# Clustered attention in slots of three steps instead of two: six PSUM banks for scores, one for all preparation

## The chip, the cores and the metric

One Trainium2 chip, one NeuronCore of it. The time is the device time of one execution in microseconds (us), the median of three runs. The engines named below are TensorE (PE; its weight loads are listed as PEld), VectorE (DVE), ScalarE (ACT), GpSimd (POOL, here a queue for transfers) and SyncE (SP, the other queue for transfers). [...]

## The reference, cut to what matters

```python
# q, k, v: (4, 8, 768, 64); centroids: (8, 16, 64); all float32
q_assign = argmax(einsum('bhsd,hcd->bhsc', q_n, c_n), -1)     # nearest centroid of each query
k_assign = argmax(einsum('bhsd,hcd->bhsc', k_n, c_n), -1)     # and of each key
mask   = q_assign[:, :, :, None] == k_assign[:, :, None, :]
scores = where(mask, q @ k^T / sqrt(64), -1e9)
attn   = softmax(scores);  x = attn @ v                       # then to (4, 768, 512)
xn  = layernorm(x) * g_ln
out = x + relu(xn @ w_ch1) @ w_ch2                            # 512 -> 2048 -> 512
```

## The kernel before, in words

**Work.** The 32 heads (4 batches of 8) are taken two at a time: 16 pairs. A pair has 768 queries in two halves of 384 (`g`) and 768 keys in six blocks of 128 (`c`), so 12 *steps* (`g`, `c`). For one step, `scores` (L373) forms a tile of 128 keys by 2 heads by 384 queries in PSUM: two bf16 matmuls lay down the mask ("far" where clusters differ), four float32 matmul records add q.k, and ACT takes the exponential into an SBUF tile `e` (L384). `weigh` (L394) multiplies the step's `e` with v into the pair's accumulator (L401), and DVE adds the `e` tiles up into `es` (L415, L418), the denominators of the softmax.

**Order.** PE, DVE and ACT run in the order written out by hand (`manual_schedule`, L606 to L670). The unit of that order is a *slot*: the score matmuls of the next two steps, then the weighing of the two steps before them; six slots are a pair. PSUM is split 4 + 1 + 3: `ps_s` holds two score tiles of two banks each, `ps_a` one accumulator, `ps_t` three banks for all else. All else is the preparation of later pairs and the finish of earlier ones:

- slot 1: `prep_sims(n+1)`, similarities of q and k to the centroids (PE L295), copied out by ACT (L304)
- slot 2: `prep_turn`, `prep_route`: transposed on PE (L311), arg-max as one-hot on DVE (L320, L322)
- slot 3: `prep_onehot`: one-hot transposed on PE (L337), `m` (L358 on ACT) and after each of the slot's score steps one `prep_mask` (L358 again)
- slot 5: `prep_transpose(n+2, ...)`: k turned by DVE (L273); q turned by PE (L278) with an ACT copy (L284) up to pair 6, by DVE from pair 7 (`TWICE = 7`). After each, the loads of pair n+3 into the same buffers are issued on the SP queue.

**Finish.** The result of a pair is divided by its denominators three stages later, because these must be spread over partitions through DRAM. `finish(n-1, 0)` in slot 0: PE sums `es` over partitions (L438), ACT copies (L446), POOL sends `flat` and fetches it back as `rdens` (L448, L449). `finish(n-1, 1)` in slot 3: DVE takes the reciprocal (L453), POOL writes `row` to DRAM (L455) and reads it back, broadcast, as `rb` (L463, two transfers). `finish(n-2, 2)` in slot 0 of the pair after: DVE multiplies `x` by `rb` (L470) and transposes (L477), SP stores. So from the reciprocal to its use the order leaves slots 3, 4, 5 and 0.

**Fillers on DVE.** In two slots of each of the first seven pairs and one slot of the later ones, a 512-column piece of the weights, which arrive as float64 words, is turned into float32: `split_weight` (three DVE instructions, L240 to L246) and, one slot later, `join_weight` (L255 to L260 and a POOL transfer L263), then the load of another piece. From pair 5 on, `extra` adds layer-norm work for the first batch of the second stage (L508, L509, L537, L539).

Second stage, from about 366 us on: the two layers of the feed-forward part as seven-product block multiplications (L711, L804). The change does not touch it.

Of the kernel before, what the change touches and what calls it, by code (L numbers as in the profile page):

```python
# [8 lines left out]
F32 = mybir.dt.float32  # L9
BF16 = mybir.dt.bfloat16  # L10
# [5 lines left out]
PSUM = bass.MemoryType.PSUM  # L16
# [3 lines left out]
def kernel(  # L20
# [35 lines left out]
    def pool(name, bufs, **kw):  # L56
        return stage.enter_context(tc.tile_pool(name=name, bufs=bufs, **kw))
# [5 lines left out]
    attn = pool("attn", 2)  # L63
    dram = ctx.enter_context(tc.tile_pool(name="dram", bufs=4, space=bass.MemoryType.DRAM))
    last = pool("last", 1)
    ps_s = pool("ps_s", 2, space=PSUM)
    ps_a = pool("ps_a", 1, space=PSUM)
    pools = {"t": pool("ps_t", 3, space=PSUM), "conv": conv}

    def ps(name, dt=F32, n=512):  # L70
        return pools["t"].tile([P, n], dt, tag="t", name=name)
# [3 lines left out]

    TWICE = 7

    blocks = {(n, name) for n in range(1, len(pairs)) for name in ("qk" if n >= TWICE else "k")}

    def load_blocks(n, name):  # L80
        b, pr = pairs[n]
# [44 lines left out]
    make_identity(nc, ident)  # L126
    identb = const.tile([P, P], BF16, name="identb")
    nc.gpsimd.tensor_copy(identb, ident)
    ones = const.tile([P, Q], F32, name="ones")
    nc.gpsimd.memset(ones, 1.0)  # L130
    rev = const.tile([P, NCL], F32, name="rev")
# [34 lines left out]
    def norm_centroids(part):  # L166
        if part == 0:
            nc.vector.tensor_tensor(c_sq, c_sb, c_sb, ALU.mult)
            nc.vector.tensor_reduce(c_ss, c_sq, AX.X, ALU.add)

            nc.vector.tensor_scalar_max(c_ss, c_ss, 2.0 ** -100)
        elif part == 1:
            nc.scalar.activation(c_nrm, c_ss, AF.Sqrt)
            nc.scalar.activation(warm, warm, AF.Exp, scale=0.0)
        else:

            nc.vector.reciprocal(c_tmp, c_nrm)
            nc.vector.scalar_tensor_tensor(
                out=c_tmp, in0=c_tmp, scalar=c_ss, in1=c_nrm, op0=ALU.mult, op1=ALU.add
            )  # L180
            nc.vector.tensor_scalar(c_nrm, c_tmp, 0.5, 1e-6, op0=ALU.mult, op1=ALU.add)
            nc.vector.reciprocal(c_tmp, c_nrm)
            nc.vector.tensor_scalar_mul(c_sb, c_sb, c_tmp)
# [5 lines left out]
    def turn_centroids():  # L189
        ct_ps = ps("ct_ps")  # L190
        nc.tensor.transpose(ct_ps[:D, : H * NCL], c_sb, ident[: H * NCL, : H * NCL])
        ct_v = ct_ps[:D, : H * NCL].rearrange("p (r j c) -> p r j c", j=2, c=NCL)
        for j in range(2):
            nc.vector.tensor_copy(cT[j * D : (j + 1) * D, :, j, :], ct_v[:, :, j, :])
# [70 lines left out]

    prepared = {n: {} for n in range(len(pairs))}

    def prep_transpose(n, side):
        src = loaded[n]["qk"[side]]
        t_sb = heads.tile([P, S], F32, tag=f"t{side}", name=f"t{side}")  # L270
        prepared[n][side] = t_sb
        if (n, "qk"[side]) in blocks:
            nc.vector.transpose(t_sb, src)  # L273
            return
        for g in range(NHALF):
            t = ps("qk_ps")
            for c in range(TH):
                nc.tensor.transpose(  # L278
                    t[:, c * P : (c + 1) * P],
                    src[:, g * TH + c, :, :].rearrange("p h d -> p (h d)"),  # L280
                    ident,
                )
            if n or g == side:
                nc.scalar.copy(t_sb[:, g * HC : (g + 1) * HC], t[:, :HC])  # L284
            else:
                nc.vector.tensor_copy(t_sb[:, g * HC : (g + 1) * HC], t[:, :HC])
# [20 lines left out]
    def prep_turn(n):  # L307
        sim_sb = prepared[n]["sim"]
        simT = ps("simT_ps")
        for c in range(TH):  # L310
            nc.tensor.transpose(  # L311
                simT[:, c * P : (c + 1) * P], sim_sb[:, c * P : (c + 1) * P], ident
            )
        prepared[n]["simT"] = simT
# [34 lines left out]
    def prep_mask(n, j):  # L349
        t, z = prepared[n]["oh"], mask[n % 2]  # L350
        src, dst = ((D, 0), (Q, D + Q))[j]
        src, dst = slice(src, src + NCL), slice(dst, dst + NCL)
        shade(n, z[dst], t[src, :S], src)
# [19 lines left out]
    def scores(i, first="mask", parts=("mask", "qk", "exp")):  # L373
        n, g, c = steps[i]
        st = prepared[n]
        if parts[0] == first:
            st["s", i] = ps_s.tile([P, 2, 512], F32, tag="s", name="s_ps")
        s = st["s", i]
        keys, cols = slice(c * P, (c + 1) * P), slice(g * HC, (g + 1) * HC)
        rows = [slice(j * D, (j + 1) * D) for j in range(2)]  # L380
        for part in parts:
            if part == "exp":
                e = attn.tile([P, 2, HC], F32, tag="e", name="e", bufs=5)
                nc.scalar.activation(e, s[:, :, :HC], AF.Exp, scale=SCALE)  # L384
                soft[i] = e
                continue
            for j in range(2):
                of_keys, of_queries = st["m"][j] if part == "mask" else [st[i][rows[j]] for i in (1, 0)]
                nc.tensor.matmul(  # L389
                    s[:, j, :HC], of_keys[:, keys], of_queries[:, cols],  # L390
                    start=part == first, stop=part != first, skip_group_check=True,
                )
# [186 lines left out]
    def put(n, slot, f, *args):  # L579
        extra.setdefault((n, slot), []).append(lambda: f(*args))  # L580

    put(5, 1, norm_load, 0)
    put(5, 2, rows_load, 0, 0)
    for t in range(NT):
        put(5 + (t + 1) // 2, (3, 5)[(t + 1) % 2], norm_rows, 0, t)
    put(9, 0, norm_stats, 0)
    put(9, 3, norm_stat_rows, 0)
    for i in range(2):
        for c in range(NDC):
            put(10 + 2 * i + c // 2, (2, 5)[c % 2], norm_apply, 0, i, c)  # L590
    put(14, 2, x_sum, 0, 1)
    put(14, 5, x_sum, 0, 2)
    put(15, 5, w1_sums, 0, 0, (0, 1))


    steps = [(n, g, c) for n in range(len(pairs)) for g in range(NHALF) for c in range(NT)]
    per = NHALF * NT
    slots = per // 2

    convert = {}  # L600
    for n in range(len(pairs)):
        for slot in (0, 3) if n < TWICE else (0,):
            convert[n, slot] = len(convert)
    order = {mybir.EngineType.PE, mybir.EngineType.DVE, mybir.EngineType.Activation}
    limit[0] = len(convert)
    with tc.manual_schedule(engines=order):  # L606
        norm_centroids(0)
        prep_transpose(0, 0)
        load(1, "q")
        norm_centroids(1)  # L610
        prep_transpose(0, 1)
        load(1, "k")
        norm_centroids(2)
        turn_centroids()
        prep_sims(0)
        prep_turn(0)
        scores(0, "qk", ("qk",))
        prep_route(0)
        load_weight(0)
        load_weight(1)  # L620
        prep_onehot(0)
        prep_mask(0, 0)
        prep_mask(0, 1)
        scores(1, "qk", ("qk",))
        scores(0, "qk", ("mask", "exp"))
        scores(1, "qk", ("mask", "exp"))
        prep_transpose(1, 0)
        load(2, "q")
        for u in range(len(pairs) * slots):
            n, slot = divmod(u, slots)  # L630
            nxt = n + 1 < len(pairs)
            if slot == 1:
                load(n + 1, "v")
            if u == 0:
                prep_transpose(1, 1)
                load(2, "k")
            if slot == 1 and nxt:
                prep_sims(n + 1)
            if slot == 2 and nxt:
                prep_turn(n + 1)  # L640
                prep_route(n + 1)
            if slot == 3 and nxt:
                prep_onehot(n + 1)
            if slot == 5 and n + 2 < len(pairs):
                prep_transpose(n + 2, 1)
                load(n + 3, "k")
                prep_transpose(n + 2, 0)
                load(n + 3, "q")
            for j in range(2):
                if 2 * u + 2 + j < len(steps):  # L650
                    scores(2 * u + 2 + j)
                if slot == 3 and nxt:
                    prep_mask(n + 1, j)
            if slot == 0 and n:
                finish(n - 1, 0)
            weigh(2 * u)
            weigh(2 * u + 1)
            if slot == (3 if nxt else 2) and n:
                finish(n - 1, 1)
            if slot == 0 and n > 1:  # L660
                finish(n - 2, 2)
            if slot == 5 and not nxt:
                finish(n - 1, 2)
            if (n, slot) in convert:
                split_weight(convert[n, slot])
            if (n, slot - 1) in convert:
                join_weight(convert[n, slot - 1])
                load_weight(convert[n, slot - 1] + 2)
            for job in extra.pop((n, slot), ()):
                job()  # L670

# [470 lines left out]
```

## Time and profile before

| | before |
|---|---|
| time, median of 3 runs | 952.06 us (951.9 to 952.77) |
| span of the profiled execution | 953.5 us |
| PE busy, instructions | 936.6 us (98%), 4614 |
| PEld busy | 574.5 us (60%) |
| DVE busy, instructions | 612.7 us (64%), 1105 |
| ACT busy | 347.6 us (36%) |
| DMA, mean busy share 0 to 100 us / 100 to 200 us | 0.6 to 0.9 / 0.88 |

A row of the costliest groups gives line, engine, operation, output<-inputs, shapes and count; then busy time and the mean of one; then the idle time of the engine just before these instructions and what ended it. In a timeline a row gives start, duration, engine, line and operation, and in brackets the idle time before it and who ended it. Ends of matmuls are modelled and overlap, so for PE the distance from start to start is the price of a block of work, not the sum of durations.

### The profile page before, as it was taken

What the parts mean: (1) busy time and instruction counts of PE and PEld (TensorE: products, weight loads), DVE (VectorE), ACT (ScalarE), POOL (GpSimd) and SP (SyncE); (2) the same over time, 40 slices, a digit from 0 to 9 for tenths busy, and PEclk for the clock granted to TensorE, in tenths of its full rate; (3) what the DMA queues carried; (4) which work ended last, traced back from release to release, by engine and by line L of the source; (5) the groups of instructions that cost most, each with busy time, mean ns of one, the idle gap of its engine ahead of it and who ended that gap; (6) DMA issues with size and microseconds to landing.
All of it is one profiled execution on the core that took longest, in us unless ns stands there. A gap on an engine that the chain in (4) does not pass through costs nothing.

```text
span 953.5 us, 12450 instructions
## 1 busy us (share of the span) xinstructions
PE 936.6 (98%) x4614; PEld 574.5 (60%) x4614; DVE 612.7 (64%) x1105; ACT 347.6 (36%) x555; POOL 79.0 (8%) x147
## 2 busy tenths in 40 slices
PE   7999999999999999999999999999999999999997
PEld 3444443444444444557887557887556887556886
DVE  4788888988888886799892436372445472344431
ACT  3666666677666663332001332001332000333000
POOL 2111111221111121110000000000000000000000
PEclk9999999999999999999999999999999999999999
DMA  8568889887877533564451002021001121000011
GB/s 175 122 150 192 194 176 205 189 194 153 178 149 158 132 69 100 137 146 144 134 159 39 1 0 78 23 89 45 0 1 58 41 84 51 1 0 7 29 45 35
DMA packets 178212, 92.48 MB, mean 97 GB/s; under 512 B 144224, under 2 KB 160720, under 8 KB 178144
## 3 DMA queue, kind: packets, MB, share of 16 engines
q1 hardware_dynamic: 168800, 76.20, 32.1%
q0 software_dynamic: 7744, 15.02, 7.9%
q8 instruction: 38, 0.62, 0.3%
q10 hardware_dynamic: 1600, 0.39, 0.2%
q14 instruction: 30, 0.25, 0.1%
HBM read 64.10 MB, written 19.10 MB: 87 GB/s over the span
## 4 chain that ended last, share of the span: by engine, by line
PE 90%; DVE 5%; issue 2%; DMA 2%; ACT 1%; POOL 0%; ACTq 0%; DVEq 0%; POOLq 0%
PE x_ps L804 17%; PE x_ps L711 16%; PE s_ps L389 15%; PE a_ps L401 12%; PE z_ps L804 9%; PE z_ps L711 8%; PE y_ps L804 4%; PE y_ps L711 4%; PE den_ps L438 1%; PE sim_ps L295 1%; DVE es L418 1%; PE simT_ps L311 1%; PE oh_ps L337 1%; PE qk_ps L278 1%; DMA rb<-row 1%
## 5 line engine op out<-in xcount | busy, mean ns | idle before, releaser
L384 ACT ACTIVATE e<-s_ps 128x768 f32<-128x768 f32 x192 | 151.6, 810 | 68.5 <-PE s_ps L389 67.7
L389 PE MATMUL s_ps<-t,t 64*128 64x384 f32 x768 | 156.5, 486 | 0.0
L401 PE MATMUL a_ps<-e,v_sb 128*64 128x384 f32 x768 | 144.8, 499 | 0.0
L418 DVE TENSOR_TENSOR es<-es,e 128x768 f32<-128x768 f32 x128 | 121.9, 952 | 24.0 <-ACT e L384 18.2
L401 PEld LDWEIGHTS a_ps<-e,v_sb 128*64 128x64 f32 x768 | 46.7, 136 | 87.7 <-issue 71.0
L731 DVE TENSOR_TENSOR h<-z_ps,u 128x384 f32<-128x384 f32 x64 | 35.6, 556 | 94.8 <-PE z_ps L711 71.5
L804 PE MATMUL x_ps<-w2t,h 128*128 128x256 f32 x384 | 84.5, 379 | 0.0
L389 PEld LDWEIGHTS s_ps<-t,t 64*128 64x128 f32 x768 | 69.0, 190 | 20.2 <-issue 18.7
L739 ACT ACTIVATE h<-h 128x384 f32<-128x384 f32 x96 | 49.6, 522 | 85.1 <-DVE h L731 85.1
L804 PEld LDWEIGHTS x_ps<-w2t,h 128*128 128x128 f32 x384 | 72.7, 190 | 10.1
L389 PE MATMUL s_ps<-m,mask 64*128 64x384 bf16 x192 | 62.9, 328 | 1.2 <-ACT e L384 1.0
L389 PE MATMUL s_ps<-mask,m 64*128 64x384 bf16 x192 | 62.7, 328 | 0.4 <-DVE mask L360 0.4
L726 ACT COPY u<-x_ps 128x384 f32<-128x384 f32 x64 | 30.6, 478 | 78.6 <-PE x_ps L711 78.6
L815 DVE TENSOR_TENSOR o_sb<-x_ps,xb 128x256 f32<-128x256 f32 x48 | 20.1, 420 | 51.3 <-PE x_ps L804 48.7
L726 ACT COPY p<-x_ps 128x384 f32<-128x384 f32 x32 | 14.9, 467 | 100.7 <-PE x_ps L711 100.7
L389 PEld LDWEIGHTS <-mask 64*128 64x128 bf16 x192 | 17.9, 93 | 54.5 <-issue 39.2
L711 PE MATMUL x_ps<-xt,ws 128*128 128x384 f32 x128 | 46.6, 487 | 0.8 <-DVE ws L574 0.8
L711 PE MATMUL x_ps<-xn,w 128*128 128x384 f32 x128 | 46.6, 487 | 0.6 <-ACT late L427 0.6
L711 PE MATMUL z_ps<-xt,ws 128*128 128x384 f32 x128 | 46.6, 487 | 0.0
L711 PE MATMUL z_ps<-xn,ws 128*128 128x384 f32 x128 | 46.5, 486 | 0.0
L711 PE MATMUL x_ps<-xn,ws 128*128 128x384 f32 x128 | 46.5, 486 | 0.0
L711 PE MATMUL x_ps<-xt,w 128*128 128x384 f32 x128 | 46.5, 486 | 0.0
(140 smaller groups left out, 1373.6 us busy)
## 6 DMA issues: line engine op xcount, KB each, us to landing
raw<-in_moe_w_ch_dram SPq DMA_DIRECT2D x32, 512.0 KB, 5.2
w<-tb POOLq DMA_DIRECT2D x32, 256.0 KB, 5.4
v_sb<-in_v_dram SPq DMA_DIRECT2D x32, 192.0 KB, 4.1
xn<-xT_d SPq DMA_DIRECT2D x16, 384.0 KB, 5.9
xr<-x_d SPq DMA_DIRECT2D x24, 256.0 KB, 3.2
xb<-x_d SPq DMA_DIRECT2D x48, 128.0 KB, 2.3
out_dram<-o_sb SPq DMA_DIRECT2D x48, 128.0 KB, 1.7
k_sb<-in_k_dram SPq DMA_DIRECT2D x62, 96.0 KB, 5.0
```

The costliest lines, as they stand in the source:

```text
L278: nc.tensor.transpose(t[:, c * P : (c + 1) * P], src[:, g * TH + c, :, :].rearrange("p h d -> p (h d)"), ident,)
L295: nc.tensor.matmul(sim[r : r + Q, :HC], cT[:, pr, :, :].rearrange("p j c -> p (j c)"), prepared[n][side][:, g * HC : (g + 1) * HC], start= ...
L384: nc.scalar.activation(e, s[:, :, :HC], AF.Exp, scale=SCALE)
L389: nc.tensor.matmul(s[:, j, :HC], of_keys[:, keys], of_queries[:, cols], start=part == first, stop=part != first, skip_group_check=True,)
L401: nc.tensor.matmul(acc[j * D : (j + 1) * D, :HC], loaded[n]["v"][:, j, c, :], e[:, j, :], start=(c == 0), stop=(c == NT - 1),)
L418: nc.vector.tensor_tensor(es, es, soft.pop(i), ALU.add)
L711: nc.tensor.matmul(bank[:, :HC], lhs[:, c, :], rhs[:, c, :], start=first and c == 0, stop=c == NDH - 1, skip_group_check=True,)
L726: nc.scalar.copy(t, bank[:, :HC])
L731: nc.vector.tensor_tensor(h, bank[:, :HC], other, ALU.add)
L739: nc.scalar.activation(h, h, AF.Relu)
L804: nc.tensor.matmul(bank[:, :MH], hidden[lhs + (c,)][:, tt * P : (tt + 1) * P], rhs[:, c, :], start=first and c == 0, stop=c == NFH - 1, sk ...
L815: nc.vector.tensor_tensor(o, bank[:, :MH], x, ALU.add)
```

## The change

The slot grows from two steps to three, so that a pair has four slots. To have three score tiles at once, `ps_s` takes six banks, and `ps_t` keeps one, so each piece of preparation waits until the one before it has been read out. The buffers of `e` go from five to seven. The work of the six slots is dealt onto four: similarities before the scores of slot 0, turning and arg-max after them; denominators (`finish 0`) in slot 1; one-hot and masks in slot 2; transposes for pair n+2 in slot 3, the PE transposes of q in two halves because only one bank is there. `finish(n-1, 1)` stays at slot 3 and `finish(n-2, 2)` at slot 0. Weight pieces are split in slots 1 and 2. Further, DVE turns pair 1's q too, the centroids' norms are finished earlier at the start and the exponential's table is loaded later, and 24 matmuls on zeros keep PE busy until the first q is there. The purpose is fewer changes between score and weighing work on PE, and a faster start.

```diff
-    ps_s = pool("ps_s", 2, space=PSUM)
+    ps_s = pool("ps_s", 3, space=PSUM)
...
-    pools = {"t": pool("ps_t", 3, space=PSUM), "conv": conv}
+    pools = {"t": pool("ps_t", 1, space=PSUM), "conv": conv}
...
-    blocks = {(n, name) for n in range(1, len(pairs)) for name in ("qk" if n >= TWICE else "k")}
+    blocks = {
+        (n, name) for n in range(1, len(pairs)) for name in ("qk" if n == 1 or n >= TWICE else "k")
+    }
...
-                e = attn.tile([P, 2, HC], F32, tag="e", name="e", bufs=5)
+                e = attn.tile([P, 2, HC], F32, tag="e", name="e", bufs=7)
...
-        for slot in (0, 3) if n < TWICE else (0,):
+        for slot in (1, 2) if n < TWICE else (1,):
...
+        idle = ps("idle_ps")
+        for _ in range(24):
+            nc.tensor.matmul(idle[:, :P], zeros, zeros, start=True, stop=True)
...
+        for side in (1, 0):
+            prep_transpose(1, side)
+            load(2, "qk"[side])
...
-            if slot == 1 and nxt:
+            if slot == 0 and nxt:
                 prep_sims(n + 1)
             if slot == 2 and nxt:
+                prep_onehot(n + 1)
+            if slot == 3 and n + 2 < len(pairs):
+                prep_transpose(n + 2, 1)
+                load(n + 3, "k")
+                prep_transpose(n + 2, 0, (0,))
+            for j in range(GROUP):
+                if GROUP * (u + 1) + j < len(steps):
+                    scores(GROUP * (u + 1) + j)
+                if slot == 2 and nxt and j < 2:
+                    prep_mask(n + 1, j)
+            if slot == 0 and nxt:
                 prep_turn(n + 1)
                 prep_route(n + 1)
...
+            if slot == (1 if nxt else 0) and n:
+                finish(n - 1, 0)
+            if slot == 3 and n + 2 < len(pairs):
+                prep_transpose(n + 2, 0, (1,))
                 load(n + 3, "q")
...
-            if slot == 0 and n:
-                finish(n - 1, 0)
-            weigh(2 * u)
-            weigh(2 * u + 1)
-            if slot == (3 if nxt else 2) and n:
+            for j in range(GROUP):
+                weigh(GROUP * u + j)
+            if slot == (3 if nxt else 1) and n:
                 finish(n - 1, 1)
             if slot == 0 and n > 1:
                 finish(n - 2, 2)
```

More of the change, by code (lines that the diff above doesn't have):

```diff
@@ L128 @@
     nc.gpsimd.tensor_copy(identb, ident)
+    zeros = const.tile([P, P], BF16, name="zeros")
+    nc.vector.memset(zeros, 0.0)
     ones = const.tile([P, Q], F32, name="ones")
@@ L173, in norm_centroids @@
             nc.scalar.activation(c_nrm, c_ss, AF.Sqrt)
-            nc.scalar.activation(warm, warm, AF.Exp, scale=0.0)
         else:
@@ L266, with prep_transpose @@
     prepared = {n: {} for n in range(len(pairs))}
-    def prep_transpose(n, side):
+    def prep_transpose(n, side, halves=range(NHALF)):
         src = loaded[n]["qk"[side]]
-        t_sb = heads.tile([P, S], F32, tag=f"t{side}", name=f"t{side}")
-        prepared[n][side] = t_sb
+        if 0 in halves:
+            prepared[n][side] = heads.tile([P, S], F32, tag=f"t{side}", name=f"t{side}")
+        t_sb = prepared[n][side]
         if (n, "qk"[side]) in blocks:
-            nc.vector.transpose(t_sb, src)
+            if 0 in halves:
+                nc.vector.transpose(t_sb, src)
             return
-        for g in range(NHALF):
-            t = ps("qk_ps")
+        if n == 0:
+            both = ps_s.tile([P, 2, 512], F32, tag="s", name="qk_ps")
+        for g in halves:
+            t = ps("qk_ps") if n else both[:, g]
             for c in range(TH):
@@ L282, in prep_transpose @@
                 )
-            if n or g == side:
+            if n or side == 0 or g == 1:
                 nc.scalar.copy(t_sb[:, g * HC : (g + 1) * HC], t[:, :HC])
@@ L582 @@
     put(5, 1, norm_load, 0)
-    put(5, 2, rows_load, 0, 0)
+    put(5, 1, rows_load, 0, 0)
     for t in range(NT):
-        put(5 + (t + 1) // 2, (3, 5)[(t + 1) % 2], norm_rows, 0, t)
+        put(5 + (t + 1) // 2, (1, 2)[(t + 1) % 2], norm_rows, 0, t)
     put(9, 0, norm_stats, 0)
-    put(9, 3, norm_stat_rows, 0)
+    put(9, 2, norm_stat_rows, 0)
     for i in range(2):
         for c in range(NDC):
[L590 to L593, printed above, removed]
+            put(10 + 2 * i + c // 2, (1, 2)[c % 2], norm_apply, 0, i, c)
+    put(14, 1, x_sum, 0, 1)
+    put(14, 3, x_sum, 0, 2)
+    put(15, 3, w1_sums, 0, 0, (0, 1))
     steps = [(n, g, c) for n in range(len(pairs)) for g in range(NHALF) for c in range(NT)]
     per = NHALF * NT
-    slots = per // 2
+    GROUP = 3
+    slots = per // GROUP
     convert = {}
     for n in range(len(pairs)):
-        for slot in (0, 3) if n < TWICE else (0,):
+        for slot in (1, 2) if n < TWICE else (1,):
             convert[n, slot] = len(convert)
@@ L610 @@
         norm_centroids(1)
+        norm_centroids(2)
         prep_transpose(0, 1)
         load(1, "k")
-        norm_centroids(2)
         turn_centroids()
+        nc.scalar.activation(warm, warm, AF.Exp, scale=0.0)
         prep_sims(0)
@@ L623 @@
         prep_mask(0, 1)
[L624 to L628, printed above, removed]
+        for i in range(1, GROUP):
+            scores(i, "qk", ("qk",))
+        for i in range(GROUP):
+            scores(i, "qk", ("mask", "exp"))
+        for side in (1, 0):
+            prep_transpose(1, side)
+            load(2, "qk"[side])
         for u in range(len(pairs) * slots):
@@ L633 @@
                 load(n + 1, "v")
-            if u == 0:
-                prep_transpose(1, 1)
-                load(2, "k")
-            if slot == 1 and nxt:
+            if slot == 0 and nxt:
                 prep_sims(n + 1)
             if slot == 2 and nxt:
+                prep_onehot(n + 1)
[9 more added lines that the diff above has]
+            if slot == 0 and nxt:
                 prep_turn(n + 1)
                 prep_route(n + 1)
[L642 to L647, printed above, removed]
-                load(n + 3, "q")
[L649 to L653, printed above, removed]
-            if slot == 0 and n:
-                finish(n - 1, 0)
-            weigh(2 * u)
-            weigh(2 * u + 1)
-            if slot == (3 if nxt else 2) and n:
+            if slot == (1 if nxt else 0) and n:
+                finish(n - 1, 0)
+            if slot == 3 and n + 2 < len(pairs):
+                prep_transpose(n + 2, 0, (1,))
+                load(n + 3, "q")
+            for j in range(GROUP):
+                weigh(GROUP * u + j)
+            if slot == (3 if nxt else 1) and n:
                 finish(n - 1, 1)
@@ L661 @@
                 finish(n - 2, 2)
-            if slot == 5 and not nxt:
+            if slot == 3 and not nxt:
                 finish(n - 1, 2)
-            if (n, slot) in convert:
-                split_weight(convert[n, slot])
             if (n, slot - 1) in convert:
@@ L668 @@
                 load_weight(convert[n, slot - 1] + 2)
+            if (n, slot) in convert:
+                split_weight(convert[n, slot])
             for job in extra.pop((n, slot), ()):
```

## The prediction

> **What bounds the kernel now.** I read the granted clock first (1.00 all through), then the busy tenths in 40 slices:
>
> ```profile
> PE   7999999999999999999999999999999999999997
> DVE  4788888988888886799892436372445472344431
> ```
>
> PE sets the time; DVE is at seven to nine tenths in the attention stage (to about 366 us). Then PE's timeline in a quiet pair (start, duration, what):
>
> ```profile
> 212.25 0.33 PE L389 MATMUL s_ps<-m,mask 64*128 64x384 bf16 x1
> ...
> 213.06 0.32 PE L389 MATMUL s_ps<-m,mask 64*128 64x384 bf16 x1
> ...
> 213.97 1.51 PE L401 MATMUL a_ps<-e,v_sb 128*64 128x384 f32 x8
> 215.41 0.33 PE L389 MATMUL s_ps<-m,mask 64*128 64x384 bf16 x1
> ```
>
> A slot of two steps is 215.41 - 212.25 = 3.16 us. The first step's scores are 0.81, the second's 0.91: 0.10 goes into the change to weighing. Weighing takes 1.44; its eight matmuls at the spacing of a step's four float32 score matmuls (0.645 for four) are 1.29, so the change back costs 0.15. Six slots are 18.96 us. Similarities add 0.78, turning 0.48, one-hot 0.44, denominators 0.78 (distances between block starts with and without them): 21.44, and the denominators' matmuls do come back every 21.46 us in most later pairs, every 22.26 where PE turns q (0.81). So PE hardly waits: excess over these prices adds up to 3.9 us in the attention stage.
>
> DVE and POOL, which seem to have room, carry a second loop. DVE's timeline in an early pair:
>
> ```profile
> 96.71 0.22 DVE L453 RECIPROCAL rdens<-rdens 128x12 f32<-128x12 f32 x1
> ...
> 102.74 0.97 DVE L273 STREAM_TRANSPOSE t<-k_sb 128x768 f32<-128x768 f32 x1
> 103.64 1.98 DVE L418 TENSOR_TENSOR es<-es,e 128x768 f32<-128x768 f32 x2
> 106.14 0.96 DVE L415 TENSOR_TENSOR es<-e 128x768 f32<-128x768 f32 x1 [0.53 <-ACT e L384]
> 109.33 0.96 DVE L470 TENSOR_TENSOR x<-x,rb 128x768 f32<-128x768 f32 x1 [2.23 <-DMA rb<-row]
> ```
>
> POOL's timeline beside it, and one row of the waits of all engines (us in total, times, longest):
>
> ```profile
> 97.23 0.57 POOL L455 DMA_DIRECT2D row<-rdens  x1 [3.88 <-DVE ta L240]
> 102.57 1.05 POOL L463 DMA_DIRECT2D rb<-row  x2 [4.77 <-issue]
> ```
>
> ```profile
> DVE x L470 <- DMA rb<-row: 6.9, 3, 2.8
> ```
>
> From the reciprocal (96.71) the denominators go to DRAM (`row`, issued 97.23, landed 102.0) and back (`rb`, landed 109.25): **L = 12.5 us**. Only then may DVE do `x`, and everything after `x` waits in DVE's order. Read from the landings, L of the finishes of pairs 1 to 11 is 8.9, 12.5, 11.9, 12.4, 9.2, 9.6, 8.1, 8.1, 8.0, 6.4, 7.2: long while weights and blocks of k are loaded, 6.3 at best. Three times DVE stood waiting (6.9 us); `x` moved 84.8, 109.3, 132.1, 155.5, up to 24.6 us apart where PE's pair is 22.26.
>
> **What the Trainium skill says.** "DMA: Bandwidth & Descriptors", Anatomy of one DMA: some 2 us fixed for a small transfer, mostly the receipt of the write, more under HBM load. The trace agrees: `row`, 6 KB, landed in 1.7 us in quiet pairs and 5.3 at worst. "Perfetto Trace Analysis", Tensor Engine Instruction: DVE and ACT are strictly first in, first out. The trace agrees: nothing passed `x` in its wait of 2.23 us. "TensorEngine Tiling (Array Packing)", Key Properties, says that a change of tiling mode drains the array; the 0.10 and 0.15 fit. "TensorE: Matmul & The Clock Gate", Part 1: the array starts at half clock until some 3.4 us of work; here the similarities take 1.51 us at the start and 0.85 later.
>
> **The change part by part.**
>
> *Slots of three, on PE.* 3 x 0.81 + 0.10 + 3 x 0.645 + 0.15 = 4.61 us; four of them 18.46, against 18.96: **-0.50 a pair**, -8 in all, if PE stays the bound.
>
> *One bank for preparation.* Q's transposes in two parts of three: 2 x 0.48 (as turning, also three) for 0.81, +0.15 in the five pairs 2 to 6. The bank's next user after the masks, and the next pair's first scores, now come one slot after the one-hot instead of two. ACT's chain there, from one-hot at 73.63: copy 73.75, m 74.25, exp 75.14, mask 75.97, exp 76.98, mask 77.81, end 78.79, so 5.16; PE's slot 2 is 0.44 + 4.61 = 5.05. PE waits 0.11 plus a signal: 0.15 a pair, 2.2 in all. Other users of the bank have two or more us in hand: the similarities are copied while three score steps (2.4) run.
>
> *Seven e, three score tiles.* Exponentials are 0.81 and a step of PE 1.45: nothing lost; queued behind them are only copies with slack.
>
> *Start.* Before, the second slot's scores begin at 18.36 with two steps scored. Now: centroids ready about 0.9 us earlier (DVE no longer does k's copy first), warm array about 1.3 (similarities 0.66, turning 0.35, one-hot 0.3), pair 1's q off PE 0.81; against that PE's similarities of pair 1 wait for two DVE transposes (1.9) and for their loads in 128-byte rows. I put pair 0's first slot at 17.1 with three steps scored; with the shorter first two pairs that is **-1.7** at pair 2; bounds 0 to -3.
>
> *The finish, which the diff leaves in "slot 3" and "slot 0".* These are now neighbours. Before, DVE had 1.39 split + 1.83 es + 1.85 join + 0.90 k + 2.94 es = 8.9 us of work between reciprocal and `x`; now it has the join (1.83), the arg-max (1.07) and two es (1.9): 4.8. The rest of L is idle DVE. From `x` to the next reciprocal DVE now has, by the start distances of 85 to 107 us: x 0.99, y 0.90, three es 2.88, split 1.37, two es 1.88, join 1.83, split 1.38, k 0.90, three es 2.88: **W = 15.0** (10.9 before). Who waits for DVE then: PE's similarities of slot 0 for the transposed k 3 us before the reciprocal, ACT's exponentials for an `e` that DVE has added (seven buffers last two slots). So a pair takes max(PE, W + L). PE has 20.94 + 0.15 = 21.1, and 22.05 where it turns q.
>
> W by pair: 15.0 for 3 and 4; with q on DVE from pair 5 (0.86) and one or two layer-norm rows (0.82 each) 16.7, 17.5 for 5, 6; with one weight piece fewer before the reciprocal (-1.38) 16.1 for 7, 15.3 for 8 and 9; with two layer-norm passes (0.95 each) 16.4 for 10 to 13. For L I take the measured values for pairs 3 to 8, since the loads they met are met again (k's load is now issued 3 us before the reciprocal, q's behind it). For 9 to 13, whose `rb` used to go before those loads, I add 1.0: pair 6's `rb`, which met k's load, took 5.4 instead of 3.4. Bounds: 6.4 everywhere, or 11.4 early and 10 late.
>
> W + L: 23.9, 27.5, 28.6, 29.9, 25.3, 24.9, 24.4, 25.5, 25.4, 23.8, 24.6 = 283.8. In pair 2 `x` still starts at its natural 6.9 us, so k is turned at 18.9. From the start of pair 2 to that of pair 14: 302.7 us. Before, 263.96 (denominator matmuls 63.82 to 327.78). **+38.7.** The last two pairs have no transposes to wait for: PE's saving, -1.0.
>
> Sum: 952.06 + 38.7 - 1.7 - 1.0 = **988**. The second stage moves as a whole.
>
> **The rivals.**
>
> *PE stays the bound* (chance 0.08): the loop is hidden. For it: PE at 98% with hardly a wait, DVE with idle time in every pair. Against it: 15.0 + 6.4 is already PE's 21.4, and W grows. Pairs 2 to 14 would be 3 x 22.05 + 9 x 21.1 = 256.1, -7.9; with start and end -10.6: **941.5**, faster.
>
> *The loop with a quiet L* (0.12): slower pairs spread the loads, and L falls to 6.4 throughout. Then two pairs at 22.05, then 22.05, 23.2, 24.0, 22.5, 21.7, 21.7, 4 x 22.8 = 270.4; +6.4 - 2.7, a little off for the loop's first slack: **955**. For it: six of sixteen L are 6.3 to 7.2. Against it: these are rows sent when no k or q load was in flight, and now always one is.
>
> *The loop at L near the measured or higher* (0.80): **988**; with 11.4 and 10 some 1000.
>
> A fourth way, a long wait of PE for the one bank (0.5 us in 15 pairs instead of 0.15), only moves the first rival to 947.
>
> **How the numbers follow.** Likeliest: 988. The range must reach from the quiet loop's region to the long L: 958 to 1006 leaves out the first rival, the lower half of the second and a tail above. Faster needs the first rival: 0.08. Within 0.2% (950.2 to 954) only the quiet loop's low end: 0.03. Slower 0.89.
>
> **What would show it.** Right: DVE's waits for `rb` grow from 6.9 us to some 60 to 80; PE's weight loads of the similarities (or ACT's exponentials) wait for DVE's transposes or sums; denominator matmuls of pairs 3 to 13 come 24 to 30 us apart; score-to-weighing changes fall from 12 to 8 a pair; the second stage is as long as before. Wrong: denominator matmuls 21 to 22 us apart, `rb` landing before DVE has done its two sums after the arg-max; or a wait of PE for ACT's masks well above 0.15 us.

## The result, and the profile after

The changed kernel takes **1009.88 us** (median of 4 runs, 1007.86 to 1012.0) against 952.32 for the kernel before in the same job: ratio 1.0605, 95% interval 1.0581 to 1.0629. It is slower, as forecast, but by 57.6 us where 36 were forecast, and the time lies just above the range's upper end of 1006. The profiled executions span 1006.1 and 953.5 us; the 52.6 us between these two are what the traces can explain. The other 5.0 us come from which executions were profiled: that of the kernel before took some 3 us more than its median, that of the changed kernel 2 us less.

The page of the kernel after: span, busy time, and the busy tenths of PE, DVE and the granted clock in 40 slices.

```profile
span 1006.1 us, 12527 instructions
PE 947.9 (94%) x4632; PEld 588.0 (58%) x4632; DVE 615.0 (61%) x1106; ACT 349.4 (35%) x554; POOL 78.0 (8%) x147
...
PE   7999888888988889899999999999999999999998
DVE  3876777777767778689988244537244645334531
...
PEclk7999999999999999999999999999999999999999
```

From slice 5 to slice 17 (some 100 to 425 us) PE now mostly stands at eight tenths where it stood at nine, and DVE is less busy too: neither is the bound. The groups of instructions of after (busy, mean, then idle before and its releaser) name what both wait for:

```profile
L408 PE MATMUL a_ps<-e,v_sb 128*64 128x384 f32 x768 | 139.6, 500 | 16.9 <-ACT x L434 16.9
...
L396 PE MATMUL s_ps<-mask,m 64*128 64x384 bf16 x192 | 64.7, 339 | 12.6 <-ACT mask L365 12.6
...
L477 DVE TENSOR_TENSOR x<-x,rb 128x768 f32<-128x768 f32 x15 | 14.4, 958 | 57.1 <-DMA rb<-row 57.1
```

The last row was 6.9 us before. One turn of the loop in DVE's timeline of after (start, duration; in brackets the idle time and who ended it):

```profile
100.40 0.96 DVE L477 TENSOR_TENSOR x<-x,rb 128x768 f32<-128x768 f32 x1 [4.71 <-DMA rb<-row]
...
115.66 0.22 DVE L460 RECIPROCAL rdens<-rdens 128x12 f32<-128x12 f32 x1
...
120.21 0.56 DVE L327 TENSOR_REDUCE best<-simT_ps 128x24 f32<-128x384 f32 x1 [2.52 <-PE simT_ps L318]
...
122.34 0.96 DVE L425 TENSOR_TENSOR es<-es,e 128x768 f32<-128x768 f32 x1
...
128.38 0.96 DVE L477 TENSOR_TENSOR x<-x,rb 128x768 f32<-128x768 f32 x1 [5.08 <-DMA rb<-row]
```

From `x` to the reciprocal DVE works 15.26 us without a gap (W); from the reciprocal to the next `x` it is 12.72 (L), of which it stands idle 7.6. Together 27.98 us a pair, where PE's own work is 22.07 (measured in the runs below where nothing waits). How the wait reaches PE is in the waits of all engines of after (us in total, times, longest):

```profile
DVE x L477 <- DMA rb<-row: 57.1, 14, 5.7
ACT x L434 <- DMA xT_d<-x: 50.3, 10, 7.2
...
PE a_ps L408 <- ACT x L434: 16.9, 10, 3.3
PE s_ps L396 <- ACT mask L365: 16.6, 16, 1.5
...
PEld qk_ps L285 <- ACT mask L365: 10.4, 5, 3.1
```

`x` late means stored late; ScalarE's copy of an accumulator waits until the `x` of two pairs earlier has left its buffer; masks and exponentials queue behind that copy, and PE behind them.

### The profile page after: what moved, and what is told of

The parts are those of the page before. It is cut to its first block, busy times and chain, and to the rows that moved or that the text cites. A ratio compares the mean times of both kernels' runs of the same rounds, so it can differ in the third digit from the quotient of the medians.

```text
span 1006.1 us, 12527 instructions
## 1 busy us (share of the span) xinstructions
PE 947.9 (94%) x4632; PEld 588.0 (58%) x4632; DVE 615.0 (61%) x1106; ACT 349.4 (35%) x554; POOL 78.0 (8%) x147
## 3 DMA queue, kind: packets, MB, share of 16 engines
q1 hardware_dynamic: 170368, 76.20, 30.9%
## 4 chain that ended last, share of the span: by engine, by line
PE 70%; DVE 9%; issue 8%; DMA 7%; ACT 4%; POOL 1%; SPq 0%; DVEq 0%; POOLq 0%; ACTq 0%
PE x_ps L818 16%; PE x_ps L725 15%; PE z_ps L818 8%; PE z_ps L725 8%; PE s_ps L396 8%; DMA rb<-row 4%; PE y_ps L818 4%; PE a_ps L408 4%; PE y_ps L725 4%; DVE es L425 3%; DMA row<-rdens 2%; ACT mask L365 2%; ACT e L391 1%; DVE x L477 1%; PE sim_ps L302 1%
## 5 line engine op out<-in xcount | busy, mean ns | idle before, releaser
L391 ACT ACTIVATE e<-s_ps 128x768 f32<-128x768 f32 x192 | 154.9, 810 | 71.0 <-PE s_ps L396 68.0
L396 PE MATMUL s_ps<-t,t 64*128 64x384 f32 x768 | 168.8, 516 | 0.0
L408 PE MATMUL a_ps<-e,v_sb 128*64 128x384 f32 x768 | 139.6, 500 | 16.9 <-ACT x L434 16.9
L408 PEld LDWEIGHTS a_ps<-e,v_sb 128*64 128x64 f32 x768 | 49.9, 137 | 94.3 <-issue 68.8
L396 PEld LDWEIGHTS s_ps<-t,t 64*128 64x128 f32 x768 | 74.0, 200 | 46.1 <-issue 46.1
L477 DVE TENSOR_TENSOR x<-x,rb 128x768 f32<-128x768 f32 x15 | 14.4, 958 | 57.1 <-DMA rb<-row 57.1
L725 PE MATMUL x_ps<-xn,ws 128*128 128x384 f32 x128 | 46.5, 486 | 0.0
L725 PE MATMUL x_ps<-xt,w 128*128 128x384 f32 x128 | 46.5, 486 | 0.0
```

Source lines behind the costliest of these rows:

```text
L396: nc.tensor.matmul(s[:, j, :HC], of_keys[:, keys], of_queries[:, cols], start=part == first, stop=part != first, skip_group_check=True,)
L408: nc.tensor.matmul(acc[j * D : (j + 1) * D, :HC], loaded[n]["v"][:, j, c, :], e[:, j, :], start=(c == 0), stop=(c == NT - 1),)
L477: nc.vector.tensor_tensor(x, x, late.pop(n), ALU.mult)
L725: nc.tensor.matmul(bank[:, :HC], lhs[:, c, :], rhs[:, c, :], start=first and c == 0, stop=c == NDH - 1, skip_group_check=True,)
```

## The experiments

The kernel before took 953.3 to 953.7 us in each of the jobs below. A run without an interval is a single one. "Pair" is the distance between the denominators' matmuls of two pairs.

**1. The loop alone, in the kernel before.** Slots of two, three banks of preparation (a bank is here a PSUM tile of 128 by 512 floats); only the reciprocal comes two slots later.

```diff
-            if slot == (3 if nxt else 2) and n:
+            if slot == (5 if nxt else 2) and n:
                 finish(n - 1, 1)
```

> The kernel before (slots of two, three banks for preparation) with the reciprocal moved from slot 3 to slot 5, next to x in slot 0. Loop theory: W becomes DVE's whole pair but one sum, about 19 us, so W + L is about 30 in the early pairs and 27 in the later ones; pairs 2 to 14 take some 335 instead of 264 us; 1010 to 1035 us. One-bank theory and x-buffer theory: nothing in their subject changes in PSUM; 952 to 960.

Measured: 1042.48 us; pairs of 24.8 to 30.9. Waits of this kernel:

```profile
DVE x L470 <- DMA rb<-row: 101.2, 15, 9.1
...
PE oh_ps L337 <- DVE onehot L322: 64.8, 13, 7.6
```

So a reciprocal too near to `x` costs 89 us with nothing else changed, more than the whole change does. The size went past the upper end of what was expected.

**2. The buffer alone.** A third `x` buffer in the changed kernel, paid for with one `e`.

```diff
-  e = attn.tile([P, 2, HC], F32, tag="e", name="e", bufs=7)
+  e = attn.tile([P, 2, HC], F32, tag="e", name="e", bufs=6)
-  xs[n] = last.tile([P, S], F32, tag="x", name="x", bufs=2)
+  xs[n] = last.tile([P, S], F32, tag="x", name="x", bufs=3)
```

> The changed kernel with three x buffers instead of two (and six e instead of seven, to make room). x-buffer theory: the 50 us in which ACT's copy of the accumulator waits for the store of an earlier x vanish and with them most of the loss: 955 to 975 us. Loop theory: that wait is only the place where DVE's lag reaches PE; it moves to another place (k's transpose, e), W + L stays, 1005 to 1015 us. One-bank theory: 1010.

Measured: 1010.67 us, ratio 1.0592 [1.0556, 1.0629], no better than without. Groups of this run:

```profile
L408 PE MATMUL a_ps<-e,v_sb 128*64 128x384 f32 x768 | 137.8, 494 | 0.0
...
L302 PE MATMUL sim_ps<-t,cT 128*32 128x384 f32 x128 | 15.2, 540 | 20.4 <-DVE t L278 19.7 <-DVE cT L197 0.7
...
L477 DVE TENSOR_TENSOR x<-x,rb 128x768 f32<-128x768 f32 x15 | 14.4, 958 | 64.9 <-DMA rb<-row 64.9
```

The 16.9 us of PE's wait for the copy are gone, and 19.7 us for k turned by DVE have come instead. The period is DVE's; at which instruction PE waits for it is secondary.

**3. The way to `x` taken out.** The changed kernel, `x` multiplied by itself; the division by the denominators is left out.

```diff
-            nc.vector.tensor_tensor(x, x, late.pop(n), ALU.mult)
+            rb = late.pop(n)
+            nc.vector.tensor_tensor(x, x, x if n + 1 < len(pairs) else rb, ALU.mult)
```

> The changed kernel with x multiplied by itself instead of by the reciprocals' copies (all pairs but the last): the division by the denominators is left out, all matmuls, DMAs and VectorE's instructions stay, and VectorE waits nowhere for the reciprocals to come back. Loop theory: VectorE's 57 us of waits are gone, pairs fall to PE's 21.1 to 22.1 us except where the store of x holds up the x buffer, time 945 to 960. If the single bank, the slots of three or VectorE's order cost the time by themselves, it stays above 990.

Measured: 963.35 us, 46.5 less than the changed kernel; the row of this multiplication:

```profile
L478 DVE TENSOR_TENSOR x<-x 128x768 f32<-128x768 f32 x15 | 14.3, 953 | 0.0
```

The wait for the reciprocals' return is thus worth 46.5 of the 57.6 us. What is left over the expected range is in pairs of 22.2 to 26.1, where the copy still waits 16.9 us for the store of `x`.

**4. and 5. The reciprocal earlier in the changed kernel**: one slot, or only ahead of slot 3's work.

```diff
-            if slot == (3 if nxt else 1) and n:
+            if slot == (2 if nxt else 1) and n:
                 finish(n - 1, 1)
```

> The changed kernel with one number changed: the reciprocal (and the transfers row and rb behind it) goes to slot 2 instead of slot 3; x stays in slot 0. Loop theory (a pair takes the larger of PE's work and W + L, W = DVE's work from x to the reciprocal, L = reciprocal to landing of rb): W falls from 15.3 to 8.1 us, W + L to about 20, under PE's 21 to 22; DVE's wait for rb falls from 57 us to under 10; the time to 944 to 952 us. One-bank theory (PE is held up because one PSUM bank serves all preparation): the bank is used as before, so 1000 us or more. x-buffer theory (ACT may not copy the accumulator out, because both x buffers wait for their store): x still comes in slot 0 but earlier, so 950 to 970.

```diff
+            if slot == 3 and nxt and n:
+                finish(n - 1, 1)
...
-            if slot == (3 if nxt else 1) and n:
+            if slot == 1 and not nxt:
                 finish(n - 1, 1)
```

> The changed kernel with the reciprocal moved only ahead of slot 3's DVE work (transpose of k, of q from pair 5, three sums), a smaller dose of the same. Loop theory: W falls by 3.9 us (4.8 from pair 5) to 11.3 in the early pairs, so with the L of the changed kernel W + L is 23.5 to 24 in the early pairs and 18 to 23 later; pairs 2 to 14 take about 268 us instead of 313; the time is 955 to 965 us, DVE's wait for rb 15 to 30 us. One-bank theory: about 1010. A saving by moving work alone, without the loop, would be near zero, as no instruction is removed.

Measured: 970.68 us (ratio 1.0167 [1.0141, 1.0194]) and 974.06 (1.0205 [1.018, 1.0231]). Both give back most of the loss, 39 and 36 us, and both miss what I expected by 9 us or more. In run 5 `row` took 4.8 us to land on average (3.2 in the changed kernel, pairs 0 to 12), since it was now issued shortly behind a weight piece's transfer in POOL's queue; run 11 shows this more clearly. In run 4, of the distances between pairs 1 to 14, eight were 21.1 to 22.1 us, the price worked out for PE, and five 23.3 to 27.8. Timeline of the worst of them:

```profile
95.06 0.95 DVE L477 TENSOR_TENSOR x<-x,rb 128x768 f32<-128x768 f32 x1
96.27 0.40 SPq L478 DMA_DIRECT2D xT_d<-x  x1
...
103.40 0.48 ACT L434 COPY x<-a_ps 128x384 f32<-128x384 f32 x1 [5.64 <-DVE es L425]
...
103.93 2.16 PE L408 MATMUL a_ps<-e,v_sb 128*64 128x384 f32 x12 [1.69 <-ACT x L434]
...
107.25 0.23 DVE L460 RECIPROCAL rdens<-rdens 128x12 f32<-128x12 f32 x1 [3.93 <-DMA rdens<-flat]
...
108.50 0.55 PE L285 MATMUL qk_ps<-ident,q_sb 128*128 128x128 f32 x3 [2.42 <-ACT mask L365]
```

`x` no longer waits, yet its store, issued at 96.27, landed at 103.30, and the copy follows at 103.40 (the bracket names a sum of DVE that happened to end then). And the reciprocal is now so early that DVE waits for the denominators' DMA. So there are two candidates for the rest, which the next runs separate.

**6. to 9. Third `x` buffer with the earlier reciprocal** (edits of 2 and 4 together), and on top of it: the reciprocal behind slot 2's conversion work; no idle matmuls at the start; pair 1's q turned by PE as before.

> The changed kernel with the reciprocal moved one slot earlier (from slot 3 to slot 2) and a third x buffer (paid for with one e buffer, 6 instead of 7). With the earlier reciprocal alone, ten of the fourteen pairs ran at PE's own 21.1 to 22.1 us and five stalled, by 5.75 + 3.4 + 5.4 + 2.2 + 4.0 = 20.8 us in all. Theory that these stalls come from the x buffers (ScalarE's copy of the accumulator at the end of slot 1 waits until the x of two pairs earlier, multiplied at the end of slot 0, has been stored; masks and exps queue behind it): with three buffers the five pairs fall to 21.1 to 22.1 us, span 948 to 955. Rival that they come from VectorE's wait for the denominators' DMA, or from the one bank of preparation, neither of which is changed: stays at 962 or more.

```diff
-            if slot == (2 if nxt else 1) and n:
+            if slot == 1 and not nxt:
                 finish(n - 1, 1)
...
             if (n, slot) in convert:
                 split_weight(convert[n, slot])
+            if slot == 2 and nxt and n:
+                finish(n - 1, 1)
```

> As the run with the earlier reciprocal and three x buffers, but the reciprocal stands behind slot 2's conversion work on VectorE instead of ahead of it: it starts some 3 to 4 us later and finds the denominators there. If VectorE's wait for the denominators (17.6 us in all with the earlier reciprocal) costs PE anything, this version is faster by 2 to 10 us. If it costs nothing, the two are equal within 2 us, as the way round (reciprocal to x) still has 3 us of slack or more; if that slack is gone, this version is slower by 3 us for each pair concerned.

```diff
-        idle = ps("idle_ps")
-        for _ in range(24):
-            nc.tensor.matmul(idle[:, :P], zeros, zeros, start=True, stop=True)
```

> As the run with the earlier reciprocal and three x buffers, without the 24 idle matmuls on zeros at the start. In the changed kernel the array ran at half speed again by the first similarities, although those matmuls had run. If they bring nothing, the first denominator's matmul starts within 0.5 us of where it starts with them; if they do keep the array quick, it starts 1.5 us later or more.

```diff
-    (n, name) for n in range(1, len(pairs)) for name in ("qk" if n == 1 or n >= TWICE else "k")
+    (n, name) for n in range(1, len(pairs)) for name in ("qk" if n >= TWICE else "k")
```

> As the run with the earlier reciprocal and three x buffers, with pair 1's q loaded as it stands and turned by PE and copied by ScalarE, as in the kernel before, instead of by VectorE from 32x32 blocks. PE's first pair gets 0.96 us more of transposes, VectorE 1 us less. The start lost 2.6 us against my forecast; if the wait for pair 1's q and k on VectorE is its reason, the first denominator's matmul starts 1 to 3 us earlier; if k alone is (it is turned by VectorE in both), it starts at the same time or up to 1 us later.

Measured: 961.22 us (1.009 [1.0071, 1.0109]) with three buffers: half of the stalls went (9.5 us), but the time stays above the 948 to 955 that the buffer alone would have given, so both candidates had a share. Timelines of DVE and PE in its worst pair, 27.0 us:

```profile
150.06 0.23 DVE L460 RECIPROCAL rdens<-rdens 128x12 f32<-128x12 f32 x1 [3.47 <-DMA rdens<-flat]
...
154.27 0.98 DVE L278 STREAM_TRANSPOSE t<-k_sb 128x768 f32<-128x768 f32 x1
...
156.16 1.51 PE L302 MATMUL sim_ps<-t,cT 128*32 128x384 f32 x8 [4.31 <-DVE t L278]
```

DVE's wait for the denominators delays k's transpose, and PE's similarities wait 4.31 us for that. The later reciprocal took 970.48 us (1.019): `x` waits for `rb` again, 26.6 us in all, so there was no slack to spend. At the start, the first denominators came at 49.54 us without the idle matmuls and at 49.53 with them: they bring nothing here. With pair 1's q on PE they came at 53.42: at this point, turning it on DVE is worth 3.9 us, where I had expected at most 1. The whole times of these two, 963.44 and 962.98 us, are single runs and too near to run 6 (959.81 to 963.75) to tell more.

**10. and 11. The denominators earlier**, ahead of slot 1's scores; and the reciprocal between join and split.

```diff
+            if slot == 1 and nxt and n:
+                finish(n - 1, 0)
...
-            if slot == (1 if nxt else 0) and n:
+            if slot == 0 and not nxt:
                 finish(n - 1, 0)
```

> As the version with the reciprocal at slot 2 and three x buffers, but the denominators' matmuls stand ahead of slot 1's score matmuls instead of behind them: 2.5 us earlier (18 score matmuls took 2.53 us), and so does ScalarE's copy, ahead of the slot's exps, and the two DMAs that the reciprocal waits for. There VectorE still waited 17.5 us in all (10 times, at most 3.5) for the denominators, and PE 10.4 us for k turned by VectorE, which stands behind that wait. If the loop (reciprocal, row, back to all partitions, x, VectorE's queue, reciprocal) is the whole story, VectorE's wait falls below 3 us, PE's below 3 us, all pairs run at 21.1 to 22.1 us, and the time is 947 to 953, at or below the kernel before. If the one bank of preparation costs something of its own (the denominators now follow the turned similarities at once in that bank), PE waits there instead and the time stays at 956 or more.

```diff
-            if slot == (2 if nxt else 1) and n:
-                finish(n - 1, 1)
...
             if (n, slot - 1) in convert:
                 join_weight(convert[n, slot - 1])
                 load_weight(convert[n, slot - 1] + 2)
+            if slot == (2 if nxt else 1) and n:
+                finish(n - 1, 1)
```

> As the run with the denominators earlier, and the reciprocal one step later in slot 2, behind the join of a weight chunk and ahead of the split of the next (some 2 us of VectorE's work). Loop theory: the way to x has slack of about 2 us, so equal within 2 us of the other where the wait for the denominators was gone already, 1 to 4 us faster where it was not.

Measured: 956.89 us (1.0039 [1.0026, 1.0052]) and 972.73 (1.0209 [1.0183, 1.0234]). The first goes the way I thought, but less far: DVE's wait for the denominators falls from 17.5 to 4.4 us, PE's for k only from 10.4 to 8.7. The time is one that I had set down for a cost of the single bank (956 or more), but the wait that goes with it is not there: what PE still waits for is k. Run 12 tests this. The second was expected equal or faster and lost 16 us. POOL's timeline of the second tells why:

```profile
126.22 0.87 POOL L266 DMA_DIRECT2D w<-tb  x1 [4.88 <-DVE rdens L460]
126.77 0.88 POOL L462 DMA_DIRECT2D row<-rdens  x1
132.14 1.06 POOL L470 DMA_DIRECT2D rb<-row  x2 [4.48 <-DMA row<-rdens]
```

Behind the join, the 6 KB of `row` follow the join's 256 KB accumulation (`w`) in one queue, and for each of pairs 0 to 12 they landed 0.2 to 0.4 us after it. From the issue of `row` to that of `rb` it took 5.4 to 6.6 us for these pairs, where the first version needs 2.4 in most. The same is seen in run 7 (4.5 to 5.9). One step later in DVE's order cost three us more on the way.

**12. k's transpose ahead of the reciprocal.**

```diff
+            if slot == 2 and n + 2 < len(pairs):
+                prep_transpose(n + 2, 1)
+                load(n + 3, "k")
             if slot == (2 if nxt else 1) and n:
                 finish(n - 1, 1)
```

(the same two lines go from slot 3).

> As the version with the reciprocal at slot 2, three x buffers and the denominators ahead of slot 1's scores; VectorE's transpose of the next pair's k now stands at the end of slot 2, ahead of the reciprocal and of the slot's conversions and row statistics, instead of at slot 3. In that version PE's only waits of the first stage's middle were 8.7 us, in four pairs (at most 3.0), for exactly this transpose, which came behind VectorE's waits for the denominators (4.4) and for a row load (2.1 in pair 5) and behind the conversions. If that is all that is left, pairs 5 to 7 fall from 24.2, 22.8 and 25.3 to 21.1 to 22.1 us, some 6 to 7 us, and the time is 948 to 951, below the kernel before (953). If VectorE has simply too much work in pairs 1 to 6 (conversion), its lateness goes to the exps' buffers or the accumulator copy instead, and the time stays at 954 to 957.

Measured: **951.55 us** (median of 22, 949.49 to 954.63) against 953.69; ratio 0.9982 [0.9973, 0.9991]: faster than the kernel before by 0.2%. The time is half a us above what I had expected. Page and groups of this version:

```profile
PE 931.2 (98%) x4632; PEld 582.0 (61%) x4632; DVE 614.4 (65%) x1106; ACT 348.5 (37%) x554; POOL 79.4 (8%) x147
...
PE   6999999999999999999999999999999999999997
...
L477 DVE TENSOR_TENSOR x<-x,rb 128x768 f32<-128x768 f32 x15 | 14.3, 953 | 1.2 <-DMA rb<-row 1.2
L302 PE MATMUL sim_ps<-t,cT 128*32 128x384 f32 x128 | 14.3, 519 | 4.8 <-DVE t L278 3.9 <-DVE cT L197 0.7
```

PE is again at nine tenths in all but the first and last slices, with the six score banks, the single bank of preparation and the slots of three all in place. They are not what made the change slow.

## Why the prediction was wrong, step by step

The mechanism held: max(PE, W + L), closed through DVE's order. Runs 1, 3, 4 and 12 show it from four sides. What failed are the sizes of terms in the sum, nearly all in one direction, and four of them above all: the start (-1.7 us forecast, +0.95 measured), L of the pairs 3 to 13 (107.3 against 111.4), and two terms that I put at nothing without a reason, the loop's hold on pair 2 (2.9) and the hand-over to the second stage (3.2). The upper end of the range came from a longer L alone (some 1000 us); the other misses came on top. In the profiled pair of executions, 52.6 us against 36:

| step of the prediction | predicted | measured | miss, us |
|---|---|---|---|
| start, at pair 2 | -1.7 | 62.10 to 63.05, +0.95 | +2.6 |
| `x` of pair 2 "at its natural 6.9 us" | 6.9 | 9.76 | +2.9 |
| W, pairs 3 to 13 | 176.5 | 178.5 | +2.0 |
| L, pairs 3 to 13 | 107.3 | 111.4 | +4.1 |
| the rest of the loop: from `rb`'s landing to `x`, W of pair 2 | 0 | some 0.1 a pair | +1.3 |
| last two pairs | -1.0 | +0.1 | +1.1 |
| "the second stage moves as a whole" | 0 | +3.2 | +3.2 |

The misses add up to 17.2 us; 0.7 of it the new kernel makes up after its last matmuls.

**Start.** I counted on a warm array: similarities 0.85 us instead of 1.51. They took 1.51 again. PE's timeline of after:

```profile
5.95 0.55 PE L285 MATMUL qk_ps<-ident,k_sb 128*128 128x128 f32 x3 [0.36 <-DMA k_sb<-in_k_dram]
7.86 0.90 PE L285 MATMUL qk_ps<-ident,k_sb 128*128 128x128 f32 x3 [1.36 <-DVE t L293]
8.55 0.42 PE L194 MATMUL ct_ps<-ident,c_sb 128*64 128x128 f32 x1
9.68 1.51 PE L302 MATMUL sim_ps<-t,cT 128*32 128x384 f32 x8 [0.70 <-DVE cT L197]
```

In this execution the array was quick at first, with three transposes in 0.55 us (six took 1.65 in the kernel before). After the wait of 1.36 us three took 0.90: the speed was lost again before the similarities, and run 8 shows that leaving the idle matmuls out changes nothing for what follows. (My reading of the granted clock, 1.00 all through, does not fit the start of the kernel before either, whose similarities took 1.51 as well.) The same wait undoes the 0.9 us that the centroids were to gain: DVE's copy of k, for which PE waits here, now stands behind the centroids' work on DVE, and PE turns the centroids (L194) at 8.55 us, where it did at 8.51. The 1.9 us allowed for waiting on DVE's transposes was more than enough (1.39). With q on PE (run 9) pair 2 would start some 5 us later than in the kernel before (0.95 and 3.9). What this consists of was not tried singly; in run 9 PE waits 1.82 and 0.57 us until ACT has read q's two halves out of the one bank, and the similarities of pair 1 then take 1.51 us too.

**The loop's first slack.** I took `x` of pair 2 as free of the loop. Its L was 11.2 us, 6.9 before at the same finish: the loop binds one pair earlier than I put it.

**L.** I reused the old landings, with 1.0 more for the late pairs. Two are off: the finishes of pairs 1 and 8, 12.24 and 11.77 us against 8.9 and 9.1. The other nine miss by up to 2.6 us either way and add up to -1.9. Why these two and not others was not tested; I think that a journey's time depends on the loads that it happens to meet, and these shift with the period. Reusing single old values was false precision, and a mean with a wider spread would have been the better input.

**End.** The hand-over to the second stage, from its first matmul to the last pair's denominators, took 7.26 us instead of 4.06: the last but one `x` stands in DVE's queue ahead of the differences of weights (`ws`) that PE needs there. It did so before too, but started 1.3 us ahead of that first matmul, and now 2.9 us behind it. Timeline at that place, after:

```profile
419.12 0.95 DVE L477 TENSOR_TENSOR x<-x,rb 128x768 f32<-128x768 f32 x1
420.21 0.48 ACT L740 COPY p<-x_ps 128x384 f32<-128x384 f32 x1 [4.08 <-DVE x L477]
...
421.99 1.53 PE L725 MATMUL x_ps<-xt,ws 128*128 128x384 f32 x4 [2.96 <-DVE ws L581]
```

DVE had worked without a gap since the `x` before (406.07, after a wait of 3.52 us for `rb`), also at splitting and joining a weight piece (3.1 us), which the kernel before does in slots 0 and 1 of the last pair. In run 12 that `x` waits 0.6 us and the hand-over takes 5.35. So the loop seems to explain part of it; that the weight piece is the rest was not tried alone. From those denominators to the last block of matmuls it is 567.2 us in both kernels, so the rest of the second stage did move as a whole.

**What was right.** PE's prices: 22.05 and 21.1 us worked out, 22.07 and 21.09 measured wherever nothing waits (run 12). From pair 2 to pair 14 that version takes 258.5 us against 263.96; my first rival had 256.1. W of the first pairs 15.26 against 15.0. The wait for `rb` came out at 57 us, a little under the 60 to 80 foretold, and the pairs 3 to 13 at 22.4 to 27.9 apart against 24 to 30. The wait for the masks, one of my signs of being wrong, did appear (16.6 us in after, some 1.0 a pair instead of 0.15). But it is no bound of its own: with the loop gone it nearly vanishes (0.4 us in run 12's score matmuls). Half right was who waits for DVE: I named the similarities and the exponentials; in after it was above all the copy into `x`'s buffer, two buffers deep, which I had not looked at. It cost nothing extra there (run 2) and 9.5 us once the loop was loosened (run 6).

## What to carry to other kernels

When slots are regrouped, go through every result that leaves an engine and comes back to it by DMA, and add up both halves: the work between the return and the next departure, and the journey. If the sum exceeds the pair's time, that engine's order sets the pace although no engine is full, and a further buffer did not help here (run 2); move the departure to an earlier slot. What then remains has to be taken one wait at a time (here buffer, source of the data, the instruction queued behind), and a small transfer should not be issued right behind a large one in the same queue.

## What the runs showed of the hardware

After short gaps PE ran at half speed for a while. In PE's timeline of after, four float32 score matmuls take 0.81 us, and 1.37 and 1.49 after two waits of 1.45 and 2.42:

```profile
102.21 0.81 PE L396 MATMUL s_ps<-t,t 64*128 64x384 f32 x4
...
104.47 2.16 PE L408 MATMUL a_ps<-e,v_sb 128*64 128x384 f32 x12 [1.45 <-ACT x L434]
109.05 0.55 PE L285 MATMUL qk_ps<-ident,q_sb 128*128 128x128 f32 x3 [2.42 <-ACT mask L365]
...
109.70 1.37 PE L396 MATMUL s_ps<-t,t 64*128 64x384 f32 x4
...
111.18 1.49 PE L396 MATMUL s_ps<-t,t 64*128 64x384 f32 x4
```

Windows of the same stretch (busy time of each engine, then the granted clock, DMA share and GB/s) show the clock falling with it:

```profile
103.00:109.00 6.00, 2.18 (x14) 0.77 (x12) 5.65 (x9) 4.95 (x6) 0.09 (x1) 1.00 0.49 83
109.00:113.00 4.00, 3.95 (x19) 2.20 (x21) 3.90 (x8) 2.27 (x4) 0.88 (x1) 0.60 0.37 88
```

The Trainium skill ("TensorE: Matmul & The Clock Gate", HAM oscillation) describes such a fall for gaps of more than some 3.4 us. Here the clock fell after two shorter ones with 2.2 us of matmuls between them. The length of a wait does not settle it: in the same trace the clock was 0.50 from 321.5 to 324.8 us, after a wait of 1.51 us at 318.8, and stayed at 1.00 from 346 to 350 us, after a wait of 1.51 us at 344.2. What decides it these runs do not show. A PE that waits therefore also works more slowly for a while: the same 4632 matmuls were busy for 947.9 us in the changed kernel and 931.2 in run 12. How much of the 57.6 us this is can't be told from the runs, since part of it falls inside waits for DVE.
